# K^T V moved behind the attention products, these done in quarter arrays, and K and V loaded ahead of Q

## Chip, cores, metric

One core of one Trainium2 chip. The metric is the device time of one execution in microseconds (us).

## The reference

```python
kv  = np.einsum('bhsd,bhse->bhde', k, v)        # 8 batches, 8 heads, 576 rows, 64 wide
out = np.einsum('bhsd,bhde->bhse', q, kv)
rms = np.sqrt(np.mean(out * out, axis=-1, keepdims=True) + 1e-06)
x   = (out / rms * g_norm)                      # then heads side by side: 4608 x 512
h   = x @ w_in                                  # 512 x 2048
g   = np.where(h > 0, h, np.exp(np.minimum(h, 0)) - 1)
return g @ w_out                                # 2048 x 512
```

Nearly all the arithmetic is in the last two matrix products; the attention is many small ones.

## The kernel before

The kernel works on nine tiles of 512 rows. Window T runs the two big products of tile T and T-1 and, in their midst, the attention of tile T+1. Every window is a list of steps in TensorE's order:

- `M3B`: the first product for two of 16 column blocks of tile T (8 full matmuls) into PSUM pair B (A, B, C are the pairs), `E3` the vector part of its elu. `R` instead of `M` lets ScalarE take the relu, which makes that vector part shorter.
- `H5`, `h0`: half of an output block of the second product for tile T-1 or T (8 full matmuls). The last half of a block is followed by ScalarE's copy, and every second block by a store.
- `K5C`: K^T V of batch 5 into pair C. `XA`: the two attention products of tile T+1 into pairs A and C, with squares, sums and inverse roots. `Y`: the scaling and the transposes of x, issued by the sync engine. `G0`, `G1`: multiply the transposed halves by g. `Q`: transposes of the next batch's q, a small copy on GpSimd (the gate) that waits until they have landed, and behind it the loads of the batch after.

```python
def fetch_ahead(b):
    raw[b] = stage.tile([P, 4, RK, D], FP32, name="st_q", tag="q")
    load(raw[b], "q", b)
    for name in "kv":
        fetch(name, b)

def kv_mm(b, kv_ps, u, ls=range(2)):            # quarter arrays: 64 rows x 64 columns
    for j in range(RK):
        for s in range(2):
            rows = slice(s * 64, s * 64 + 64)
            for l in ls:
                nc.tensor.matmul(kv_ps[s][l * 64 : l * 64 + 64, u * 64 : u * 64 + 64],
                    lhsT=bf["k", b][rows, 2 * l + u, j, :], rhs=bf["v", b][rows, 2 * l + u, j, :],
                    start=(j == 0), stop=(j == RK - 1))

def se_mm(T, h, se_ps):                         # half arrays, quarters where two batches meet
    for i in range(2):
        (b0, j0), (b1, j1) = (slot_of(T, 4 * h + 2 * i + t) for t in range(2))
        parts = [(0, P, b0, j0, 2)] if b0 == b1 else [(0, 64, b0, j0, 1), (64, P, b1, j1, 1)]
        ...                                     # for m, for l, for part: one matmul of 64 columns

steps = "M0B K5C H1 E0 M1A H3 E1 M2B H4 E2 H5 XA Y H6 Q M3B H7 E3 M4A E4 M5C E5 M6B G0 E6 M7A G1 E7 h0 h2"   # window 4
```

Of the kernel before, what the change touches and what calls it, by code (L numbers as in the profile page):

```python
# [8 lines left out]
FP32 = mybir.dt.float32  # L9
# [7 lines left out]
def kernel(  # L17
# [14 lines left out]
    P = 128  # L32

    B, H, S, D = q.shape
    DM = H * D
    DF = moe_w_in.shape[1]
    RK = S // 64
# [5 lines left out]
    V, A, Q = nc.vector, nc.scalar, nc.gpsimd  # L43

    const = ctx.enter_context(tc.tile_pool(name="const", bufs=1))
    stage = ctx.enter_context(tc.tile_pool(name="stage", bufs=1))
# [28 lines left out]
    def slot_of(T, n):  # L75
        return divmod(8 * T + n, RK)

    bf, raw = {}, {}
    src_of = {"q": q, "k": k, "v": v}

    def fetch(name, b, u=None):

        if (name, b) not in bf:
            bf[name, b] = qkvp.tile([P, 4, RK, D], BF16, name=f"{name}_bf", tag=name)
        ms = slice(0, 4) if u is None else slice(u, 4, 2)
        load(bf[name, b][:, ms], name, b, ms)

    def load(dst, name, b, ms=slice(0, 4), eng=nc.gpsimd):
        in_ = src_of[name][b].rearrange("h r d -> (h r d)").rearrange("(m p x) -> p m x", m=4, p=P)
        eng.dma_start(out=dst.rearrange("p m j d -> p m (j d)"), in_=in_[:, ms, :])  # L90

    def fetch_ahead(b):
        raw[b] = stage.tile([P, 4, RK, D], FP32, name="st_q", tag="q")
        load(raw[b], "q", b)
        for name in "kv":
            fetch(name, b)

    def cast_q(b):

# [67 lines left out]
    def kv_of(b, l, u, s):  # L167
        return kv_sb[l * 64 : l * 64 + 64, b, u, s]
# [11 lines left out]
    def y_mm(T, u, ps, ls=range(2)):  # L180

        n = 0
        while n < 8:
            b, j = slot_of(T, n)
            m = min(8 - n, RK - j)
            for l in ls:
                for s in range(2):
                    nc.tensor.matmul(  # L188
                        ps[l][s * 64 : s * 64 + 64, n * 64 : (n + m) * 64],
                        lhsT=kv_of(b, l, u, s),  # L190
                        rhs=qT[b][l * 64 : l * 64 + 64, s, u, j : j + m, :],
                        start=True,
                        stop=True,
                    )
            n += m
# [19 lines left out]
    class Turned:  # L215
# [7 lines left out]
        def product(self, y):  # L223
            self.y = y
            y_mm(self.T, self.u, y)
# [11 lines left out]
        def scale(self, l):  # L237
            scale_t(self.T, self.y[l], self.r[:, l, :], 2 * l + self.u)

    def se_mm(T, h, se_ps):  # L240

        for i in range(2):
            (b0, j0), (b1, j1) = (slot_of(T, 4 * h + 2 * i + t) for t in range(2))
            parts = [(0, P, b0, j0, 2)] if b0 == b1 else [(0, 64, b0, j0, 1), (64, P, b1, j1, 1)]
            for m in range(4):
                u, s = m // 2, m % 2
                for l in range(2):
                    for lo, hi, b, j, n in parts:
                        nc.tensor.matmul(  # L249
                            se_ps[lo:hi, l, (4 * i + m) * 64 : (4 * i + m) * 64 + 64],  # L250
                            lhsT=qT[b][l * 64 : l * 64 + 64, s, u, j : j + n, :],
                            rhs=kv_of(b, l, u, s),
                            start=True,
                            stop=True,
                        )

    def kv_all(b, tag):
        kv_ps = pair(tag, "kv_ps")
        for u in range(2):
            kv_mm(b, [kv_ps[:, s, :] for s in range(2)], u)  # L260
        return lambda: nc.scalar.copy(
            kv_sb[:, b], kv_ps[:, :, 0:P].rearrange("p s (u e) -> p u s e", u=2)
        )

    def attention(T):

        st = {}

        def se(h):
            def product(tag="C"):  # L270
                st["se", h] = pair(tag, "se_ps")
                se_mm(T, h, st["se", h])

            def square():
                sq = attp.tile([P, 2, DM], BF16, name="sq", tag="sq")
                nc.scalar.activation(sq, st["se", h], AF.Square)  # L276
                st["sq", h] = sq

            def sums():
                ss = attp.tile([P, 2 * H], FP32, name="ss", tag="ss")  # L280
                st["ss", h] = ss
                nc.vector.reduce_sum(  # L282
                    out=ss,
                    in_=st.pop(("sq", h)).rearrange("p l (m e) -> p (l m) e", e=D),
                    axis=AX.X,
                )

            def inv():
                ss = st["ss", h]
                nc.scalar.activation(ss, ss, AF.Ln, bias=eps_col, scale=1.0 / D)  # L290
                nc.scalar.activation(ss, ss, AF.Exp, scale=-0.5)  # L291

            def scale():
                if h == 0:
                    st["xs"] = attp.tile([P, J, DM], BF16, name="xs", tag="xs")
                    x_tile(T)
                se_ps, ss = st.pop(("se", h)), st.pop(("ss", h))
                nc.vector.tensor_tensor(  # L298
                    out=st["xs"][:, 2 * h : 2 * h + 2, :].rearrange("p i (l m e) -> p l i m e", l=2, e=D),
                    in0=se_ps.rearrange("p l (i m e) -> p l i m e", i=2, e=D),  # L300
                    in1=ss.rearrange("p (l i m) -> p l i m", l=2, i=2).unsqueeze(4).to_broadcast([P, 2, 2, 4, D]),
                    op=ALU.mult,
                )
                for i in (2 * h, 2 * h + 1):
                    nc.sync.dma_start_transpose(
                        out=xT[T][:, :, i * P : i * P + P], in_=st["xs"][:, i, :]
                    )

            def gain():
                cols = slice(2 * h * P, 2 * h * P + 2 * P)  # L310
                nc.vector.tensor_scalar(  # L311
                    out=xT[T][:, :, cols],
                    in0=xT[T][:, :, cols],
                    scalar1=g_col,
                    scalar2=None,
                    op0=ALU.mult,
                )

            return product, square, sums, inv, scale, gain

        pieces = {}
        for h in range(2):
            for name, piece in zip(("se", "sq", "sum", "inv", "mul", "gain"), se(h)):
                pieces[f"{name}{h}"] = piece
        return pieces
# [124 lines left out]
    def mm2_half(T, i):  # L450
        mm2(T, i // 2, 8 * (i % 2), 8 * (i % 2) + 8)
# [90 lines left out]
    y_ps, sq0 = {}, {}  # L542
# [217 lines left out]
    def window(T, steps):  # L760





        rest = {}
        nxt = attention(T + 1) if T + 1 < NT else None
        for step in steps.split():
            kind, arg = step[0], step[1:]
            if kind in "MR":  # L770
                i, tag = int(arg[0]), arg[1]
                make = mm1_rest if T == 2 and i == 0 else mm1
                rest[i] = make(T, i, tag, kind == "R")
            elif kind == "E":
                rest.pop(int(arg))()
            elif kind == "H":
                mm2_half(T - 1, int(arg))
            elif kind == "h":
                mm2_half(T, int(arg))
            elif kind == "K":  # L780
                kv_all(int(arg[0]), arg[1])()
            elif kind == "X":
                nxt["se0"](arg)
                nxt["se1"]("C")
                for name in ("sq0", "sq1", "sum0", "sum1", "inv0", "inv1"):
                    nxt[name]()
            elif step == "Y":
                nxt["mul0"]()
                nxt["mul1"]()
            elif step == "Q":  # L790
                b = T + 2
                if b < B:
                    turn_q(b)
                if b + 1 < B:
                    after_turn(b)
                    fetch_ahead(b + 1)
            elif kind == "G":
                nxt[f"gain{arg}"]()
            else:
                raise ValueError(step)  # L800
# [4 lines left out]
    for T in range(2, NT):  # L805
        if T + 2 < B:
            cast_q(T + 2)
        if T == 2:
            steps = "M0B K3C E0 M1A H5 E1 M2B E2 R3A H6 E3 XB Y H7 Q M4A E4 h0 R5B E5 M6C G0 E6 M7A G1 E7 h2"
        elif T + 1 < NT:  # L810
            kv = f"K{T + 1}C" if T + 1 < B else ""
            steps = (
                f"M0B {kv} H1 E0 M1A H3 E1 M2B H4 E2 H5 XA Y H6 Q M3B H7 E3 M4A E4 M5C E5 M6B G0 E6 M7A G1 E7 h0 h2"
            )
        else:
            steps = "M0B H1 E0 M1A H3 E1 M2B H4 E2 M3A H5 E3 M4B H6 E4 M5A H7 E5 M6B E6 M7A E7 h0 h2"
        window(T, steps)
# [33 lines left out]
```

## Time and profile before

| | before |
|---|---|
| median of the runs in the first comparison | 284.10 us |
| span of the core in the profile | 282.2 us |
| PE busy | 273.3 us, 97% |
| waits of PE for another engine after 50 us | none listed |

The span runs from the core's first instruction to its last; the time adds some 1.8 us around it. PE is TensorE's matmuls. Two figures from single matmul starts are used throughout: the **cost of a piece** (last full matmul before it to a full one after it, less 216 ns per full step) and the **inner distance**, from the last full matmul before window 2's product to that before window 7's: 142.17 us before. It leaves out the start of the kernel, which the change does not touch and which shifts by up to 0.6 us between traces.

### The profile page before, as it was taken

What the parts mean: (1) busy time and instruction counts of PE and PEld (TensorE: products, weight loads), DVE (VectorE), ACT (ScalarE), POOL (GpSimd) and SP (SyncE); (2) the same over time, 40 slices, a digit from 0 to 9 for tenths busy, and PEclk for the clock granted to TensorE, in tenths of its full rate; (3) what the DMA queues carried; (4) which work ended last, traced back from release to release, by engine and by line L of the source; (5) the groups of instructions that cost most, each with busy time, mean ns of one, the idle gap of its engine ahead of it and who ended that gap; (6) DMA issues with size and microseconds to landing.
All of it is one profiled execution on the core that took longest, in us unless ns stands there. A gap on an engine that the chain in (4) does not pass through costs nothing.

```text
span 282.2 us, 5145 instructions
## 1 busy us (share of the span) xinstructions
PE 273.3 (97%) x2094; PEld 129.2 (46%) x2123; DVE 163.9 (58%) x222; ACT 141.6 (50%) x209; POOL 49.1 (17%) x89
## 2 busy tenths in 40 slices
PE   8799999999999999999999999999999999999994
PEld 3444444444544444444444444444444444444443
DVE  2549532967457736864587448834893489344600
ACT  3778359594566445533552445344543464333311
POOL 7743303322033033034003400000000000000000
PEclk9999999999999999999999999999999999999999
DMA  7999999999999969579437954612180215030222
GB/s 207 201 204 206 206 258 238 196 254 121 173 277 178 155 186 232 99 193 261 108 74 175 268 130 42 148 49 74 37 114 0 74 40 112 0 77 1 74 74 74
DMA packets 50571, 39.46 MB, mean 140 GB/s; under 512 B 30964, under 2 KB 44020, under 8 KB 50548
## 3 DMA queue, kind: packets, MB, share of 16 engines
q0 software_dynamic: 15008, 21.30, 37.6%
q1 hardware_dynamic: 35136, 17.31, 29.9%
q10 hardware_dynamic: 404, 0.53, 0.6%
q8 instruction: 16, 0.26, 0.3%
q14 instruction: 7, 0.06, 0.1%
HBM read 36.70 MB, written 9.44 MB: 163 GB/s over the span
## 4 chain that ended last, share of the span: by engine, by line
PE 92%; DMA 3%; POOL 1%; issue 1%; ACT 1%; DVE 1%; POOLq 0%; DVEq 0%
PE h_ps L381 42%; PE o_ps L402 42%; DMA v_bf<-in_v_dram 3%; PE kv_ps L155 2%; PE se_ps L249 2%; PE h_ps L568 1%; PE o_ps L439 1%; POOL k_bf L90 1%; PE qt_ps L173 0%; PE mean L198 0%; PE y_ps L188 0%; POOL v_bf L90 0%; ACT elu_e L349 0%; DVE xT L211 0%; POOL q_bf L90 0%
## 5 line engine op out<-in xcount | busy, mean ns | idle before, releaser
L402 PE MATMUL o_ps<-w_out_sb,gT 128*128 128x512 bf16 x542 | 127.1, 379 | 1.5 <-issue 1.0
L381 PE MATMUL h_ps<-xT,w_in_sb 128*128 128x512 bf16 (+1 forms) x551 | 125.5, 376 | 0.6
L349 ACT ACTIVATE elu_e<-h_ps 128x1024 bf16<-128x1024 f32 (+1 forms) x79 | 73.9, 951 | 73.0 <-PE h_ps L381 71.6
L381 PEld LDWEIGHTS <-w_in_sb 128*128 128x128 bf16 x560 | 54.5, 98 | 64.5 <-issue 0.9
L402 PEld LDWEIGHTS <-gT 128*128 128x128 bf16 x560 | 53.5, 98 | 64.0 <-issue 0.9
L365 DVE TENSOR_TENSOR gT<-elu_e,h_ps 128x1024 bf16<-128x1024 bf16 (+1 forms) x67 | 77.2, 1157 | 6.9 <-DVE elu_e L361 0.5
L361 DVE TENSOR_SCALAR elu_e<-elu_e 128x1024 bf16<-128x1024 bf16 x72 | 32.0, 445 | 59.1 <-ACT elu_e L349 59.0
L418 ACT COPY o_sb<-o_ps 128x512 f32<-128x512 f32 x32 | 18.3, 586 | 30.8 <-PE o_ps L402 30.8
L103 POOL CAST q_bf<-st_q 128x384 bf16<-128x384 f32 x36 | 18.0, 544 | 39.1 <-DMA st_q<-in_q_dram 34.4
L282 DVE TENSOR_REDUCE ss<-sq 128x16 f32<-128x1024 bf16 x14 | 16.5, 1214 | 13.0 <-ACT sq L276 13.0
L298 DVE TENSOR_TENSOR xs<-se_ps,ss 128x1024 bf16<-128x1024 f32 x14 | 16.5, 1216 | 1.2 <-ACT ss L291 1.2
L276 ACT ACTIVATE sq<-se_ps 128x1024 bf16<-128x1024 f32 x14 | 13.7, 1030 | 0.3 <-PE se_ps L249 0.3
L211 DVE SCALAR_TENSOR_TENSOR xT<-y_ps,g_col,rT 128x512 bf16<-128x512 f32 (+1 forms) x10 | 6.2, 640 | 10.1 <-ACT rT L208 8.0
L338 POOL COPY gate<-qT 1x16 bf16<-1x16 bf16 x5 | 0.9, 186 | 57.3 <-DMA qT<-q_bf 57.3
L354 ACT ACTIVATE elu_h<-h_ps 128x1024 bf16<-128x1024 f32 (+1 forms) x12 | 9.3, 817 | 0.0
L155 PEld LDWEIGHTS <-k_bf 64*64 64x64 bf16 x576 | 6.3, 107 | 5.3 <-issue 5.3
L155 PE MATMUL kv_ps<-v_bf,k_bf 64*64 64x64 bf16 x576 | 7.5, 194 | 1.0 <-DVE v_bf L112 0.5
L90 POOL DMA_DIRECT2D v_bf<-in_v_dram x11 | 7.7, 698 | 4.0 <-DMA w_in_sb<-in_moe_w_in_dram 2.1
L90 POOL DMA_DIRECT2D k_bf<-in_k_dram x11 | 7.8, 705 | 2.7 <-DMA w_in_sb<-in_moe_w_in_dram 2.0
L290 ACT ACTIVATE ss<-ss,eps_col 128x16 f32<-128x16 f32 x14 | 4.3, 307 | 6.7 <-DVE ss L282 6.7
L365 DVE TENSOR_TENSOR gT<-elu_e,elu_h 128x1024 bf16<-128x1024 bf16 x9 | 6.6, 739 | 1.6 <-ACT elu_h L354 0.9
L311 DVE TENSOR_SCALAR xT<-xT,g_col 128x1024 bf16<-128x1024 bf16 x14 | 6.7, 481 | 1.2 <-DMA xT<-xs 1.2
(56 smaller groups left out, 92.9 us busy)
## 6 DMA issues: line engine op xcount, KB each, us to landing
st_q<-in_q_dram POOLq DMA_DIRECT2D x6, 1152.0 KB, 7.9
out_dram<-o_sb SPq DMA_DIRECT2D x24, 256.0 KB, 3.3
k_bf<-in_k_dram POOLq DMA_DIRECT2D x6, 576.0 KB, 10.4
v_bf<-in_v_dram POOLq DMA_DIRECT2D x6, 576.0 KB, 12.7
out_dram<-o_sb SPq DMA_DIRECT2D x19, 128.0 KB, 2.4
w_out_sb<-in_moe_w_out_dram POOLq DMA_DIRECT2D x4, 512.0 KB, 15.1
w_in_sb<-in_moe_w_in_dram POOLq DMA_DIRECT2D x2, 512.0 KB, 10.8
q_bf<-in_q_dram POOLq DMA_DIRECT2D x3, 288.0 KB, 13.6
```

Source lines behind the costliest of these rows:

```text
L90: eng.dma_start(out=dst.rearrange("p m j d -> p m (j d)"), in_=in_[:, ms, :])
L103: nc.gpsimd.tensor_copy(out=bf["q", b][:, u, js], in_=raw[b][:, u::2, js, :].rearrange("p l j d -> p j l d"),)
L155: nc.tensor.matmul(kv_ps[s][l * 64 : l * 64 + 64, u * 64 : u * 64 + 64], lhsT=bf["k", b][rows, 2 * l + u, j, :], rhs=bf["v", b][rows, 2 * ...
L276: nc.scalar.activation(sq, st["se", h], AF.Square)
L282: nc.vector.reduce_sum(out=ss, in_=st.pop(("sq", h)).rearrange("p l (m e) -> p (l m) e", e=D), axis=AX.X,)
L298: nc.vector.tensor_tensor(out=st["xs"][:, 2 * h : 2 * h + 2, :].rearrange("p i (l m e) -> p l i m e", l=2, e=D), in0=se_ps.rearrange("p l ...
L349: nc.scalar.activation(e[:, lo:hi, :], h, AF.Exp)
L361: nc.vector.tensor_scalar(out=e, in0=e, scalar1=1.0, scalar2=1.0, op0=ALU.min, op1=ALU.subtract)
L365: nc.vector.tensor_tensor(out=gT[T][:, 2 * i + lo : 2 * i + hi, :], in0=e[:, lo:hi, :], in1=h, op=ALU.add if relu else ALU.max,)
L381: nc.tensor.matmul((ps[a] if isinstance(ps, list) else ps[:, a, :])[:, cols], lhsT=w_in_sb[:, c, f * P : f * P + P], rhs=xT[T][:, c, cols] ...
L402: nc.tensor.matmul(o_ps[T, j], lhsT=gT[T][:, f, j * P : j * P + P], rhs=w_out_sb[:, f, :], start=(f == 0), stop=(f == FC - 1),)
L418: nc.scalar.copy(o_sb[T, half][:, j % 2, :], o_ps[T, j])
```

## The change

The intent is to spare TensorE its changes of array mode. K^T V of batches 5 to 7 goes directly behind the two attention products of windows 3 to 5, one window earlier than it was, and the products there (and in the even windows, where a pair of rows crosses a batch) use quarter arrays all through. K and V are then wanted a window earlier, so they are loaded ahead of their Q.

```diff
-    def fetch_ahead(b):
-        raw[b] = stage.tile(...); load(raw[b], "q", b)
-        for name in "kv":
-            fetch(name, b)
+    def fetch_ahead(b, order="qkv"):
+        for name in order: ...
-            parts = [(0, P, b0, j0, 2)] if b0 == b1 else [(0, 64, b0, j0, 1), (64, P, b1, j1, 1)]
+            parts = [(0, 64, b0, j0, 1), (64, P, b1, j1, 1)]
+            if b0 == b1 and not quarters:
+                parts = [(0, P, b0, j0, 2)]
             elif kind == "X":
-                nxt["se0"](arg)
-                nxt["se1"]("C")
+                quarters = len(arg) > 1 or T % 2 == 0
+                nxt["se0"](arg[0], quarters)
+                nxt["se1"]("C", quarters)
+                nxt["sq0"]()
+                if len(arg) > 1:
+                    kv_all(int(arg[1]), arg[2])()
-                    fetch_ahead(b + 1)
+                    fetch_ahead(b + 1, "kvq")
+        elif T == 3:
+            steps = "M0B K4C H1 E0 M1A H3 E1 M2B H4 E2 M3A H5 E3 H6 XB5A Y H7 Q M4A E4 h0 M5B E5 M6C G0 E6 M7A G1 E7 h2"
         elif T + 1 < NT:
-            kv = f"K{T + 1}C" if T + 1 < B else ""
-            steps = f"M0B {kv} H1 E0 M1A ... H5 XA Y H6 Q M3B ... h0 h2"
+            kv = f"{T + 2}B" if T + 2 < B else ""
+            steps = f"M0B H1 E0 M1A ... H5 XA{kv} Y H6 Q M3B ... h0 h2"
```

(The code is shortened: the calls after K^T V are the squares, sums and inverse roots as before. The step lists are cut at the dots; the rest of them is unchanged.)

More of the change, by code (lines that the diff above doesn't have):

```diff
@@ L90, in load @@
         eng.dma_start(out=dst.rearrange("p m j d -> p m (j d)"), in_=in_[:, ms, :])
-    def fetch_ahead(b):
-        raw[b] = stage.tile([P, 4, RK, D], FP32, name="st_q", tag="q")
-        load(raw[b], "q", b)
-        for name in "kv":
-            fetch(name, b)
+    def fetch_ahead(b, order="qkv"):
+        for name in order:
+            if name == "q":
+                raw[b] = stage.tile([P, 4, RK, D], FP32, name="st_q", tag="q")
+                load(raw[b], "q", b)
+            else:
+                fetch(name, b)
     def cast_q(b):
@@ L238, in scale, with se_mm @@
             scale_t(self.T, self.y[l], self.r[:, l, :], 2 * l + self.u)
-    def se_mm(T, h, se_ps):
+    def se_mm(T, h, se_ps, quarters=False):
         for i in range(2):
             (b0, j0), (b1, j1) = (slot_of(T, 4 * h + 2 * i + t) for t in range(2))
-            parts = [(0, P, b0, j0, 2)] if b0 == b1 else [(0, 64, b0, j0, 1), (64, P, b1, j1, 1)]
+            parts = [(0, 64, b0, j0, 1), (64, P, b1, j1, 1)]
+            if b0 == b1 and not quarters:
+                parts = [(0, P, b0, j0, 2)]
             for m in range(4):
@@ L269, in se, with product @@
         def se(h):
-            def product(tag="C"):
+            def product(tag="C", quarters=False):
                 st["se", h] = pair(tag, "se_ps")
-                se_mm(T, h, st["se", h])
+                se_mm(T, h, st["se", h], quarters)
             def square():
@@ L782, in window @@
             elif kind == "X":
-                nxt["se0"](arg)
-                nxt["se1"]("C")
-                for name in ("sq0", "sq1", "sum0", "sum1", "inv0", "inv1"):
+                quarters = len(arg) > 1 or T % 2 == 0
[4 more added lines that the diff above has]
+                    kv_all(int(arg[1]), arg[2])()
+                for name in ("sq1", "sum0", "sum1", "inv0", "inv1"):
                     nxt[name]()
@@ L809 @@
             steps = "M0B K3C E0 M1A H5 E1 M2B E2 R3A H6 E3 XB Y H7 Q M4A E4 h0 R5B E5 M6C G0 E6 M7A G1 E7 h2"
+        elif T == 3:
+            steps = "M0B K4C H1 E0 M1A H3 E1 M2B H4 E2 M3A H5 E3 H6 XB5A Y H7 Q M4A E4 h0 M5B E5 M6C G0 E6 M7A G1 E7 h2"
         elif T + 1 < NT:
-            kv = f"K{T + 1}C" if T + 1 < B else ""
-            steps = (
-                f"M0B {kv} H1 E0 M1A H3 E1 M2B H4 E2 H5 XA Y H6 Q M3B H7 E3 M4A E4 M5C E5 M6B G0 E6 M7A G1 E7 h0 h2"
-            )
+            kv = f"{T + 2}B" if T + 2 < B else ""
+            steps = f"M0B H1 E0 M1A H3 E1 M2B H4 E2 H5 XA{kv} Y H6 Q M3B H7 E3 M4A E4 M5C E5 M6B G0 E6 M7A G1 E7 h0 h2"
         else:
```

## The prediction

> **What bounds the kernel now.** I read the page's busy row first, then the waits of TensorE over the steady part, then the chain that ended last, and last the single matmul starts.
>
> ```profile
> span 282.2 us, 5145 instructions
> PE 273.3 (97%) x2094; PEld 129.2 (46%) x2123; DVE 163.9 (58%) x222; ACT 141.6 (50%) x209; POOL 49.1 (17%) x89
> PEclk9999999999999999999999999999999999999999
> ```
>
> 97% busy alone would prove little. The wait list of PE from 50 us to the end does:
>
> ```profile
> engine line waited for: us in total, times, longest us
> PE o_ps L402 <- issue: 0.8, 5, 0.2
> ```
>
> In 232 us PE waits for no other engine long enough to be listed. So what the change adds to or takes from PE's stream shows one to one in the time, unless it makes a new wait. The chain (start, duration, work) shows the pieces concerned:
>
> ```profile
> 108.13 0.57 PE se_ps L249 x32
> ...
> 124.35 1.73 PE h_ps L381 x8
> 126.07 0.71 PE kv_ps L155 x72
> 126.78 0.16 issue
> 126.94 1.67 PE o_ps L402 x7
> ...
> 137.24 0.81 PE se_ps L249 x40
> ```
>
> L155 is K^T V of a batch (72 matmuls, 64x64 arrays), alone between full matmuls. L249 is the attention product (both halves of a tile): 32 matmuls on 64x128 half arrays, or 40 where a pair of rows crosses a batch, 16 of which are on 64x64 quarters between half-array ones.
>
> Single starts in the trace give the rates. Full matmuls: 216 ns apart. Half arrays: two in 29 ns. Quarters: four in 32 ns (8 each). A change of mode costs a start-to-start of 120 to 125 ns; from a full matmul to a small one it is 309 to 312 ns instead of 216. What a piece costs is the distance from the last full matmul before it to a full one after it, less 216 ns per full step (a few records are missing and are counted in):
> - K^T V alone: 811 ns = 96 entry + 582 for its 72 + 133 exit (windows 4, 5, 6 alike).
> - product on halves, no crossing (windows 3, 5): 680 ns.
> - product with a crossing: 915 and 916 ns (windows 2, 4), 809 in window 6, where the quarters come last and one switch is saved.
>
> **What the Trainium skill says.** "TensorEngine Tiling (Array Packing)", Key Properties: changing the tiling mode drains the array, changing only the tile does not. The trace agrees: 120 to 125 ns at a switch against 26 within a mode. "TensorE: Matmul & The Clock Gate", Part 3, says small tiles of different row groups overlap and start about 4 ns apart; here the four of a quarter group start 3 to 4 ns apart, the groups 32 ns. "DMA: Bandwidth & Descriptors", Issuing engines are not separate DMA queues: all DMAs share 16 engines and interleave. The trace agrees: with an output store in flight, K and V packets land at 48 to 60 per 0.5 us (108 to 110.5 us), without one at 83 to 93 (111 to 112.5). The two mode rules are why the change can pay, the last is its risk.
>
> **The change, part by part.**
> It removes the separate K^T V of batches 5, 6, 7 (3 x 811 ns), puts the same matmuls behind the products of windows 3, 4, 5, and makes the products of windows 2 to 6 all quarters: 64 instead of 32 or 40 small matmuls, 136 more in all. At 8 ns a quarter, 64 need what 32 halves need, so doubling the count is free. Taking the K^T V figure as template: 64 quarters alone (8 fewer) cost 811 - 8 x 8 = 747 ns; 64 + 72 cost 811 + 64 x 8 = 1323 ns.
> - Window 2: 915 to 747, -168.
> - Window 3: 680 + 811 to 1323, -168.
> - Window 4: 916 + 811 to 1323, -404.
> - Window 5: 680 + 811 to 1323, -168.
> - Window 6: 809 to 747, -62.
> - Sum: **-0.97 us**, all on PE, which is the path.
>
> ACT's copy of K^T V (0.37 us) now sits between the two squares. The vector work needs the first square and then 1.2 us for its sum, so the second sum starts about when it did: no cost.
>
> Added wait 1, end of window 3. Its new order puts the product late, as window 2 has it, with only seven groups of eight full matmuls after it. Window 2 already pays for this:
>
> ```profile
> 94.49 0.48 DVE L311 TENSOR_SCALAR xT<-xT,g_col 128x1024 bf16<-128x1024 bf16 x1
> ...
> 95.07 1.89 PE L381 MATMUL h_ps<-xT,w_in_sb 128*128 128x512 bf16 x8
> ```
>
> The last gain ends at 94.97, the next window's first matmul starts at 95.07, 456 ns after the one before it instead of 216: 0.24 us of waiting. Window 3 gets no relu form for its tile 5, so the product of that elu takes 1.22 us on DVE instead of 0.69. Counted from the first product matmul: tile 5's exp at 8.32, min 9.38, product 9.90, gain 11.04, min 11.43, product 11.96, second gain 13.10 to 13.58, matmul at 13.68; PE would be ready at 13.31. **+0.37 us**, in a window that had no such wait.
>
> Added wait 2, K and V of batch 6 in window 4. Loads go out when GpSimd's gate sees Q's transposes landed:
>
> ```profile
> 99.73 0.19 POOL L338 COPY gate<-qT 1x16 bf16<-1x16 bf16 x1 [12.28 <-DMA qT<-q_bf]
> ...
> 122.13 0.19 POOL L338 COPY gate<-qT 1x16 bf16<-1x16 bf16 x1 [11.56 <-DMA qT<-q_bf]
> ```
>
> ```profile
> 92.31 1.29 SPq L460 DMA_DIRECT2D out_dram<-o_sb  x2
> 93.69 3.73 SPq L330 DMA_TRANSPOSE qT<-q_bf  x2
> ...
> 118.42 2.83 SPq L330 DMA_TRANSPOSE qT<-q_bf  x2
> ```
>
> In window 2 a store goes just ahead of the transposes and the gate opens 6.0 us after their issue; in window 3, with the store behind them, 3.7 us. In the new order of window 3 the eighth half (H7), hence its store, comes ahead, so I take 6.0. Window 3's first product matmul: 94.90 + 72 x 0.2158 + 0.81 + 0.10 = 111.34 us. In window 2 the gate came 17.7 us after that point, so here at 129.0; K goes out at 129.6, first packets 2.3 us after that (as 100.27 to 102.5 showed), 1024 packets of K and V at 85 to 90 per 0.5 us take 5.8 us, and the next tile's store from about 134.3 on takes some 1.2 us more: V lands at 138 to 139.2. Window 4 wants it at 125.02 + 56 x 0.2158 + 0.10 + 0.52 = 137.7. So **0 to 1.5 us** of waiting; loading K and V ahead of Q is what keeps it from being several. Batch 5 has about 2 us to spare (V landed near 109.5 to 110, wanted at 111.9), batch 7 about 5. Q lands last but is cast long before its transposes.
>
> Sum without wait 2: 284.08 - 0.97 + 0.37 = 283.48. With 0.8 us of it: 284.3.
>
> **The rivals.**
> (a) Pure PE arithmetic, both waits absent: 283.1. For it: everything listed of PE's waits is tiny, and the odd order of window 3 looks made to let batch 5 land. Against it: window 2's own 0.24 us wait has the same cause.
> (b) The load of batch 6 comes late by its full estimate or more: 284.9 to 285.3. For it: both windows with a store ahead of Q's transposes (gates at 77.15 and 99.73) took 6.0 us, the three others 3.6 to 3.7. Against it: about 1.1 us of these 6.0 is a pause of the transposes that may not recur, and the estimate's errors are as large as the wait.
> (c) Quarters lose: K^T V's stationary operand, or the second bank, brings a pause between product and K^T V, 0.1 us at each of three places: +0.3. Both use the same four arrays in the same order, so I give it little.
>
> **Range and chances.** Between 283.5 (no late load) and 284.3 (late by 0.8) I lean slightly to the middle: **283.9 us**. Range 283.1 (rival a) to 285.1 (rival b). No path reaches 2% (5.7 us): faster 0.01, same 0.98, slower 0.01.
>
> **What would show it.** Right: the K^T V groups of batches 5 to 7 gone as separate pieces; in the chain a product of 64 and K^T V of 72 in one stretch of some 1.1 us in windows 3, 4 and 5, quarters at 8 ns each; no 120 ns jump inside windows 2 to 6. Wait 1: a gap of about 0.4 us at window 4's first h_ps matmul, released by DVE L311. Wait 2: PE kv_ps waiting on a v_bf or k_bf DMA near 137.7 us; the gate near 129 confirms its cause, a gate near 127 refutes it. Wrong would be: a quarter rate well off 8 ns when the moving operand is kv_sb in long runs, a wait on PSUM tile A or B in window 3 (I count 1 us of slack for the bank of tile 3), or a load that misses batch 5 as well.

## The result, and the profile after

284.43 us (284.34 to 285.28, 4 runs) against 284.10 (283.95 to 284.42, 4 runs). The ratio is 1.0017, interval 0.9996 to 1.0038: the same within 2%, slightly slower if anything. Ratios here are the mean time of one kernel's runs over that of the other's of the same rounds, so not quite the ratio of the medians quoted.

The waits of PE after 50 us, in the kernel after:

```profile
engine line waited for: us in total, times, longest us
PE o_ps L407 <- issue: 0.5, 3, 0.2
PE h_ps L386 <- DVE xT L316: 0.2, 1, 0.2
```

L316 is the multiplication by g. That is a wait on another engine, which the kernel before did not have in this list. The chain of the kernel after shows where (start, duration, work):

```profile
111.81 0.64 PE se_ps L254 x64
112.45 0.74 PE kv_ps L157 x72
113.20 0.16 issue
113.36 1.67 PE o_ps L407 x7
...
123.89 0.06 DVE gT L370
123.95 1.08 issue
125.03 0.49 DVE xT L316
125.52 0.05 issue
125.57 1.90 PE h_ps L386 x8
...
137.83 0.64 PE se_ps L254 x64
138.47 0.04 issue
138.51 0.77 PE kv_ps L157 x72
```

The first lines are the new piece in window 3: 64 quarter matmuls of the product with the 72 of K^T V behind. In the middle the chain leaves PE for DVE: the first matmul of window 4 starts 560 ns after the matmul before it, 344 more than the usual 216. In the last lines there is a hole ahead of K^T V of batch 6. The views name no releaser for so short a hole, but the semaphores' times do. K^T V starts 61 ns after the product's last matmul where it waits for nothing (window 5). In window 3 it was 158: 15 of the 16 completion updates of V's load had come by 111.81 us, the last at 112.29. In window 4 it was 229: 15 by 137.70, the last at 138.38.

| ns | before | forecast | after |
|---|---|---|---|
| window 2, product | 915 | 747 | 748 |
| window 3, product and K^T V of 5 | 680 + 811 | 1323 | 1491, of which 97 for V |
| window 4, product and K^T V of 6 | 916 + 812 | 1323 | 1561, of which 168 for V |
| window 5, product and K^T V of 7 | 680 + 811 | 1323 | 1397 |
| window 6, product | 809 | 747 | 746 |
| wait for the gain, window 4 | 0 | 370 | 344 |

The sums are 6434 before and 6287 after: 0.15 us less, and the inner distance is 142.03 us, 0.14 less. So this trace's middle is a little faster; its window 2 began 0.40 us later for reasons ahead of the change, and its span is 282.5 us. Of the 0.97 us that the forecast saves on PE only 0.14 arrived. The experiments ask what the rest depends on.

### The profile page after: what moved, and what is told of

It reads as the page before. It is cut to its first block, busy times and chain, and to the rows that moved or that the text cites. A ratio compares the mean times of both kernels' runs of the same rounds, so it can differ in the third digit from the quotient of the medians.

```text
span 282.5 us, 5417 instructions
## 1 busy us (share of the span) xinstructions
PE 273.9 (97%) x2229; PEld 129.6 (46%) x2259; DVE 163.0 (58%) x222; ACT 142.0 (50%) x209; POOL 48.2 (17%) x89
## 4 chain that ended last, share of the span: by engine, by line
PE 94%; DVE 2%; issue 2%; ACT 1%; DVEq 0%
PE o_ps L407 42%; PE h_ps L386 41%; PE kv_ps L157 2%; PE se_ps L254 2%; PE kv_ps L529 2%; PE h_ps L573 1%; PE o_ps L444 1%; PE qt_ps L175 1%; ACT elu_e L354 1%; PE mean L200 1%; PE y_ps L190 1%; DVE elu_e L366 0%; DVE xT L316 0%; DVE kv_sb L114 0%; DVE xT L213 0%
## 5 line engine op out<-in xcount | busy, mean ns | idle before, releaser
L366 DVE TENSOR_SCALAR elu_e<-elu_e 128x1024 bf16<-128x1024 bf16 x72 | 31.0, 431 | 59.0 <-ACT elu_e L354 58.9
L105 POOL CAST q_bf<-st_q 128x384 bf16<-128x384 f32 x36 | 16.7, 508 | 61.0 <-DMA st_q<-in_q_dram 55.6
L316 DVE TENSOR_SCALAR xT<-xT,g_col 128x1024 bf16<-128x1024 bf16 x14 | 6.9, 491 | 1.8 <-DMA xT<-xs 1.8
## 6 DMA issues: line engine op xcount, KB each, us to landing
out_dram<-o_sb SPq DMA_DIRECT2D x19, 128.0 KB, 2.4
```

The source lines that it names most:

```text
L105: nc.gpsimd.tensor_copy(out=bf["q", b][:, u, js], in_=raw[b][:, u::2, js, :].rearrange("p l j d -> p j l d"),)
L366: nc.vector.tensor_scalar(out=e, in0=e, scalar1=1.0, scalar2=1.0, op0=ALU.min, op1=ALU.subtract)
```

## The experiments

Each edit is relative to the kernel after, unless it says otherwise. All results were correct. "Before" is the kernel before on the same chip, 11 runs per batch: 284.07, 284.08 and 284.17 us median in the three batches.

### after_again: no edit

> The changed kernel as it is, beside the others on the same chip. My theory: TensorE's stream is 0.9 us shorter, and 0.7 to 0.8 us of it is given back by three waits that the change makes: the first matmul of window 4 waits about 0.34 us for the second gain of xT, and K^T V of batches 5 and 6 wait 0.1 and 0.2 us for the last of V. So 0.0 to 0.3 us over the kernel before, with these waits in the trace again, the two for V of varying length. Rival (run-to-run start only): the waits are not there again and the time equals before less 0.9.

284.99 us (283.72 to 285.77), ratio 1.0033 (1.0015 to 1.0052). The profiled run was the shortest; in its trace batch 5 waited for nothing (60 ns), batch 6 began 206 ns after the product, the gain was waited for as before, and the inner distance was 141.91 us. The waits are there, and the unprofiled runs are 1 to 2 us longer than the profiled one. The kernel before never scattered so: 283.76 to 284.39.

### quarters_only: the products alone

```diff
 # relative to before: quarters in windows 2 to 6, all else as before
+ quarters = T < 7
```

> The kernel before with nothing but the quarter arrays in the products of windows 2 to 6; K^T V, the loads and the order of window 3 are as before. My sum of mode switches says -168 (window 2), +67 (3), -169 (4), +67 (5), -62 (6) = -0.27 us against before, products of 747 ns each. Rival: twice as many small matmuls cost time in themselves; then windows 3 and 5 lose 0.3 us each and the total is not below before.

Each of the five products cost 745 to 748 ns, and the inner distance was 141.90 us, 0.26 under before: the sum held. A view of its chain:

```profile
108.06 0.64 PE se_ps L254 x64
```

This stands against x32 in 0.57 us for window 3 before. Twice the matmuls take 67 ns more by the starts (747 against 680 ns), so windows 3 and 5 lose and only the three crossings gain. The timed runs did not show the 0.26: 284.10 us, ratio 1.0005 (0.9993 to 1.0017). Its spans had a mean of 282.12 against 282.27, and the time outside the span was 1.76 to 2.72 us against 1.74 to 1.82 in before; the last section comes back to this.

### turn_before_store: Q's transposes ahead of the store

```diff
-"... XB Y H7 Q M4A ..."    "... XB5A Y H7 Q M4A ..."     # windows 2 and 3
+"... XB Y Q H7 M4A ..."    "... XB5A Y Q H7 M4A ..."
```

> The changed kernel with Q's transposes issued ahead of half H7 (and so ahead of its store) in windows 2 and 3. If the late V is due to the gate that waits behind the store, the gates come 3.7 us after the transposes' issue instead of 5 to 6, K and V land 2 us earlier and both waits of K^T V vanish: 0.3 us under the changed kernel, the wait for the gain (0.34) stays. Rival: the 16 DMA engines are simply full, the store then falls into the loads, V lands no earlier and the waits stay.

Two lines of the timeline of window 3 in the kernel after (start, duration, engine, work), and the same two of this one:

```profile
123.58 3.52 SPq L335 DMA_TRANSPOSE qT<-q_bf  x2
...
128.57 0.47 POOL L343 COPY gate<-qT 1x16 bf16<-1x16 bf16 x1 [10.70 <-DMA qT<-q_bf]
```

```profile
121.75 2.80 SPq L335 DMA_TRANSPOSE qT<-q_bf  x2
...
125.46 0.19 POOL L343 COPY gate<-qT 1x16 bf16<-1x16 bf16 x1 [8.86 <-DMA qT<-q_bf]
```

The gate comes 3.7 us after the transposes' issue instead of 5.0 (in window 2, 3.6 instead of 6.3). So the store ahead does delay the transposes. But beside after_again, whose window 2 began within 0.06 us of this one, V of batch 6 was issued 2.5 us earlier and landed only 1.1 us earlier (136.70), and V of batch 5 was issued 3.9 earlier and landed 0.9 earlier (110.71): the store now runs beside the loads. In the trace the waits for V were gone (78, 60 and 61 ns), inner distance 141.78. The time was 284.26 us (283.63 to 286.32), ratio 1.0018 (0.9994 to 1.0042): both theory and rival got a part right, and the scatter stayed.

### only_6_7: batch 5 and window 3 as before

```diff
-steps = "M0B K4C ... M3A H5 E3 H6 XB5A Y H7 Q ... h2"      # window 3
+steps = "M0B K4C H1 ... H5 XA Y H6 Q ... h0 h2"            # window 3 as before
+"M0B K5C H1 ..."                                           # window 4: batch 5 alone
```

> Only batches 6 and 7 are moved behind the products of windows 4 and 5; window 3 keeps the order and the halves of before, and batch 5 stays alone at the start of window 4. By my sum: window 2 -0.17, window 4 -0.33, window 5 -0.09, window 6 -0.06 = -0.65 us against before, no wait for the gain in window 4 and none for V. Rival: if moving K^T V behind the product saves nothing in itself, the result stays within 0.2 us of before.

283.48 us (283.24 to 283.54, and one run of 284.80 with a span of 283.0), ratio 0.9987 (0.9971 to 1.0003): the median is 0.59 under before, but the interval still takes in no change. The inner distance was 141.53 us, 0.635 under before, against 0.65 by the sum. V of batch 6 landed at 134.66, wanted at 137.7: window 3's gate opens early when its store is behind the transposes. No wait for the gain in window 4. So in the trace moving batches 6 and 7 pays what the arithmetic says, and what costs goes with batch 5 and window 3's new order. The one long run was not traced; V of batch 6 had 3 us to spare in the run that was, so a late V is no ready reason for it.

### q_load_first: the old order of loads

```diff
-fetch_ahead(b + 1, "kvq")
+fetch_ahead(b + 1, "qkv")
```

> The changed kernel with the old order of loads (Q, then K, V) in the windows. If the load of V stands right at the edge, V of batch 5 lands near 114.5 us (as in the kernel before) against 112.2 wanted, and V of batch 6 near 142 against 138.2 plus the delay so far: K^T V waits about 2.3 and 4 us, the time is 5 to 7 us over the changed kernel, some 290 us. Rival: V has slack and the spread of the changed kernel has another cause; then the order of loads changes under 1 us.

293.60 us, ratio 1.0334 (1.0320 to 1.0349): worse than forecast. Waits of PE, and the granted clock (the column after the engines) in two stretches of this kernel:

```profile
PE kv_ps L157 <- DMA v_bf<-in_v_dram: 5.5, 2, 3.0
```

```profile
core 0: us, PE busy (x) PEld busy (x) DVE busy (x) ACT busy (x) POOL busy (x), PEclk, DMA share, GB/s
114.50:118.50 4.00, 3.67 (x79) 1.84 (x81) 1.84 (x2) 2.23 (x6) 0.00 (x0) 0.58 0.01 4
119.00:125.00 6.00, 6.00 (x29) 2.74 (x28) 2.79 (x4) 2.42 (x3) 0.00 (x0) 1.00 0.43 87
```

V of batch 5 landed at 114.36 us and K^T V began 2.73 us after the product; in window 4, 3.17 us. The waits were forecast, their price was not: after each, the granted clock was 0.50 for 3.41 us (from 115.16 and from 145.88 us; the 0.58 above is the mean of a stretch that begins before it), and eight full matmuls took 427 ns apiece instead of 216, about 1.7 us more per wait. The Trainium skill, "TensorE: Matmul & The Clock Gate", Why this matters for your kernels, says to leave no PE gaps over about 3 us between bursts, or the clock goes back to half; here 2.73 us from start to start, some 2.5 us of it idle, was enough, while gaps of 1.94 and 1.61 us (gain_earlier and both_mended) left the clock at 1.00. The load order in the change is therefore worth about 9 us: without it the move would have been a clear loss.

### gain_earlier: the second gain ahead of the sixth elu

```diff
-"... M6C G0 E6 M7A G1 E7 h2"      # windows 2 and 3
+"... M6C G0 G1 E6 M7A E7 h2"
```

> The changed kernel with the second gain issued ahead of the sixth elu's vector work in windows 2 and 3. My theory: the waits of 0.24 us (window 3's first matmul) and 0.34 us (window 4's) vanish, so 0.58 us under the changed kernel of the same rounds, the waits for V stay or grow by what PE arrives earlier (up to 0.58 us given back to them). Rival: the gain waits for its transposes instead, the gaps stay as they are.

284.80 us (284.45 to 286.19), ratio 1.0036 (1.0017 to 1.0056). Both gaps at the first matmuls of windows 3 and 4 vanished. But PE then came to K^T V of batch 6 earlier, and V came later (139.11). The chain of this trace goes straight from the load to K^T V:

```profile
129.20 9.91 DMA v_bf<-in_v_dram
139.11 0.14 issue
139.24 0.77 PE kv_ps L157 x72
```

K^T V began 1.94 us after the product. Most of that is one of the load's 16 completions: fifteen had come by 137.76, the last at 139.11. The 0.58 us saved were more than given back: the load did not come earlier for it, so taking away the wait ahead of it gained nothing.

### kv_window_earlier and kv_earlier_gain: K and V one window earlier still

```diff
-qkvp = ... tc.tile_pool(name="qkvp", bufs=3)
+qkvp = ... tc.tile_pool(name="qkvp", bufs=4)
 # fetch_ahead(4) loads batch 4 and K, V of 5; later ones load Q of b and K, V of b + 1
+        if 4 <= b < B - 1:
+            for name in "kv":
+                fetch(name, b + 1)
 # kv_earlier_gain: also the edit of gain_earlier
```

> The changed kernel with K and V loaded one window earlier still (a fourth buffer for each), so that neither can be waited for; the wait for the gain is left in. My theory: K^T V of batches 5 to 7 starts 61 ns after the product in each window (a semaphore instruction remains), the distance from window 2's product to window 7's is 141.7 us against 142.17 before, the time is about 0.4 us under before and the spread of the runs (283.7 to 285.8 for the changed kernel) shrinks to that of before (some 0.6 us). Rival: the spread and the loss come from elsewhere, and both stay.

> Both mends: K and V one window earlier, and the second gain ahead of the sixth elu in windows 2 and 3. My sum: -0.97 of the change, -0.24 of the wait that the kernel before has in window 3, +0.2 for three semaphore instructions: 1.0 us under before, 283.1 us. Rival: what is taken away shows up as another wait (transposes for the gain, loads that collide with stores), under 0.5 us of gain.

291.20 us, ratio 1.0269 (1.0248 to 1.0290), and 290.01, ratio 1.0216 (1.0198 to 1.0235). The waits for V were gone, as the theory said: product and K^T V together cost 1397 ns in windows 3 to 5 of the first one. But the extra loads (K and V of batch 5 on top of the three of batch 4) filled the DMA engines just when x is transposed for window 3. Waits of PE in kv_window_earlier, and the gain's line there:

```profile
PE h_ps L389 <- DVE xT L319: 5.7, 2, 5.5
```

```profile
97.76 0.49 DVE L319 TENSOR_SCALAR xT<-xT,g_col 128x1024 bf16<-128x1024 bf16 x1 [5.35 <-DMA xT<-xs]
```

One gain idled 5.35 us for its transposes (landing took up to 9.3 us, median 2.5), PE 5.5 us behind it, and the clock fell again. This experiment removed one wait and made another, so it cannot say where the scatter comes from; its runs lie 2.1 us apart with no wait for V in the trace. The rival of kv_earlier_gain (collisions) won.

### after_third: no edit

> The changed kernel a third time, for the spread and for one more trace. In the traces so far K^T V of batch 6 began 229 and about 200 ns after the product (61 is the least), while most unprofiled runs were 0.5 to 1.5 us longer. Theory: the same wait for V of batch 6, of 0 to 2 us; so runs between 283.7 and 286, and the profiled run's time over the shortest equals its gap before that K^T V. Rival: a long run shows no such gap.

284.54 us (283.79 to 285.31), ratio 1.0014 (0.9999 to 1.0028). The profiled run was once more the shortest: K^T V began 98 ns after the product in window 3, 248 in window 4. No long run of the kernel after itself was caught in a trace.

### only_5_7: batch 6 alone taken back

```diff
-kv = f"{T + 2}B" if T + 2 < B else ""
+kv = "7B" if T == 5 else ""
+"M0B K6C H1 ..."                    # window 5: batch 6 alone
```

> The changed kernel with batch 6 alone taken back (its K^T V stands at the start of window 5, in no hurry for its V); window 3 keeps its new order with batch 5. My sum: -168 (window 2), -94 (3), -168 (4), -94 (5), -62 (6), +343 for the gain = -0.24 us against before, with 0 to 0.2 us for V of batch 5; and if V of batch 6 makes the spread, the runs lie within some 0.6 us of each other as before's do. Rival: batch 5 or something else makes the spread: it stays 1.5 us or more and the time at 284.5 or over.

284.24 us (283.79 to 285.53), ratio 1.0016 (0.9998 to 1.0035). The inner distance was 141.925 us, 0.241 under before: the sum to a hundredth. But the scatter stayed, with spans of 281.9 to 283.6. So V of batch 6 is not its only source. V of batch 5 is another candidate: it landed at 111.40 us for 111.7. But the traced run had no wait, so that is not shown.

### only_6_7_gain: only 6 and 7, and the gain earlier in window 2

```diff
 # only_6_7, and in window 2:
-"... M6C G0 E6 M7A G1 E7 h2"
+"... M6C G0 G1 E6 M7A E7 h2"
```

> Batches 6 and 7 moved, window 3 as before, and in window 2 the second gain issued ahead of the sixth elu's vector work, which takes away the 0.24 us that the kernel before waits too. My sum: -0.65 - 0.24 = -0.89 us against before, 283.2 us, the fastest of all. Rival: the 0.24 us come back at another wait; then it is as only_6_7 was, 0.6 us under before.

283.30 us (283.11 to 283.37), ratio 0.9969 (0.9957 to 0.9980): 0.9 us under before, the fastest of all and with the least scatter. The inner distance is 141.27 us, 0.895 less than before, against 0.89 by the sum. Its timeline of the gain in window 2 and the next matmul:

```profile
93.62 0.48 DVE L316 TENSOR_SCALAR xT<-xT,g_col 128x1024 bf16<-128x1024 bf16 x1 [0.70 <-DMA xT<-xs]
...
94.84 1.89 PE L386 MATMUL h_ps<-xT,w_in_sb 128*128 128x512 bf16 x8
```

The gain now idles 0.70 us for its transposes, but ends 0.74 us ahead of the matmul, and PE no longer waits.

### both_mended: all three batches, store and gain mended

```diff
 # the edits of turn_before_store and gain_earlier together
```

> The changed kernel with all three batches moved, Q's transposes ahead of H7's store and the second gain earlier, both in windows 2 and 3. By the traces V of batch 6 then lands at 136.7 us against 137.3 wanted, V of batch 5 at 110.7 against 111.6: my sum is -0.97 - 0.24 + 0.2 = -1.0 us against before in a run with no wait, but with only 0.6 us to spare and a landing that scatters by 1 us many runs should lose up to 1 us, so a median near 283.7 and a spread over 1 us. Rival: the traces' slack holds and all runs lie near 283.1.

284.83 us (283.87 to 286.79), ratio 1.0026 (1.0002 to 1.0051). The scatter is over 1 us as expected, the median worse than expected. In its trace V of batch 6 landed at 138.76 us, 2 us later than in turn_before_store although issued 0.2 earlier, and K^T V began 1.61 us after the product. For this load a landing is uncertain by more than the slack that these orders give it. The run of 286.79 us was not traced, but its granted clock is 0.994, where every other run of these orders but q_load_first and the two with K and V a window earlier has 0.997 or more; the traced run of kv_earlier_gain, with one stretch at half clock behind a gap, has 0.993. That points to a long gap of PE in it, and does not show which.

## Why the prediction was right or wrong

The time lay in the range: 283.9 forecast, 284.43 measured, 283.1 to 285.1 given. The direction did not: 0.2 us under before was forecast, 0.33 over was measured, and part of that comes from outside the core's span, for which the prediction has no term. By its own steps:

- **PE's stream, -0.97 us.** Right for the products alone (748 and 746 ns against 747). For product and K^T V it was 1397 against 1323 ns: K^T V starts 61 ns after the product's last matmul where a step of 8 was assumed, and the 64 quarters take 525 ns from first start to last, not 504. So the stream alone gives -0.75, not -0.97. A semaphore instruction of 51 ns stands in PE's queue in that pause; that it makes the pause was not tested. This is the size of rival (c), to which little was given: its 0.1 us per place was near the 0.074 measured, though its two reasons were not tested either. The sentence that doubling the count is free was wrong by the prediction's own figures (64 quarters at 8 ns are 512 ns, 32 halves at 14.5 are 464), but its sum used 747 against 680 and so was not touched. (By the starts K^T V alone is 93 + 582 + 136 ns, not 96 + 582 + 133; its 811 is right.)
- **Wait 1, +0.37 us for the gain.** Right: 0.34 in all three traces of the kernel after. The cause is shown by gain_earlier, which removes it.
- **Wait 2, 0 to 1.5 us for V of batch 6.** The mechanism was right, shown by the semaphores' times, by q_load_first and by the chain of gain_earlier. That the landing fitted (137.8 to 138.4 us for 138 to 139.2) is partly luck: the gate came at 128.0 to 128.6 instead of 129.0, because the transposes took 4.9 to 5.0 us behind the store and not 6.0, and the first packets came at 130.0 to 130.5 instead of 131.9, but the packets then took 7.4 to 7.6 us and not 5.8, or 7.0 with a store beside them. In the kernel's own traces the wait was 0.15 to 0.19 us, where the forecast leant on 0.8; in two edited orders that reach K^T V earlier it was 1.55 and 1.88.
- **"Batch 5 has about 2 us to spare"** was wrong. V landed at 111.6 to 112.3 us, not at 109.5 to 110. The first packets came at 102.0 to 102.5, as counted on, but the 1024 packets of K and V took 9.1 to 9.5 us: 48 to 57 per 0.5 us in the first 3 us, and 42 to 53 for some 2 us beside a store, where the prediction counts 85 to 90 for batch 6. It stood at the edge: 0 to 0.1 us of wait in the traces.
- **What the timed runs add.** The 16 runs of the kernel after have a mean span of 282.64 us against 282.32 for 33 runs of before. A run with no wait for V would have, by the corrected sum, about 282.32 - 0.75 + 0.34 = 281.9, which is the shortest span seen. So 0.74 us on average are lost beyond the shortest. That this is V in every long run was argued from the two edited orders; no long run of the kernel after was traced, and the long runs of only_6_7 and only_5_7 speak against V of batch 6 as the only source. The time outside the span adds 0.3 us on average that nothing in the prediction had; its cause stays open.

So where did the gain go? 0.22 us was never there, 0.34 went into the gain's wait that the new order of window 3 brings, and in the three traces 0.15 to 0.27 into V of batches 5 and 6, which land just as they are wanted. What the rest of the 0.74 us and the 0.3 us outside the span come from is not shown.

## What to carry to other kernels

Count what a regrouping of small matmuls saves from single starts: in four traces here sums of 0.24 to 0.89 us held to two hundredths of a microsecond. But a consumer moved a window earlier is only as fast as its load. Measure the load's landing over several runs: here landings of one load in nearly equal orders lay 2 us apart, and 3 us of slack left no wait in the two traces that had it. Taking back the one move without slack, and window 3's new order with it, turned a loss of 0.1 to 0.3% into a saving of 0.1% that is not clear of noise; with the multiplication by g issued earlier in window 2 as well it became 0.3%, which is. And when two waits follow one another on the same engine and the later one is for a load that does not depend on the earlier, removing the earlier one only lengthens the later, as in gain_earlier.

## What the Trainium skill lacked or had wrong

- "TensorEngine Tiling (Array Packing)", Key Properties, says that a change of mode drains, without a size. Here: 118 to 127 ns from start to start instead of 26 to 32; 309 to 312 instead of 216 when coming from a full matmul.
- "TensorE: Matmul & The Clock Gate", Back-to-back issue gap, gives about 25 ns as the least step for a matmul of up to 64 columns. The starts on one tile were 29 to 32 ns apart here; but over four quarters in rotation the mean step was 8 ns, over two halves 14.5.
- The same page, Why this matters for your kernels, puts the limit for PE gaps at about 3 us: a gap of 2.73 us from start to start (some 2.5 us idle) was followed by 3.41 us at half clock; gaps of 1.94 and 1.61 us were not.
- No page gives a size for the scatter of one load's 16 completions: the last came 0.48 and 0.68 us after the fifteenth in the two late loads of the kernel after, 1.35 us in gain_earlier.
- No page says what a store queued ahead of transposes within SBUF costs: 4.9 to 6.3 us from issue to the gate instead of 3.6 to 3.7.
- No page explains why the time outside the core's span varies: 1.73 to 1.83 us in 33 runs of the kernel before and at most 1.84 in 11 runs of only_6_7 and only_6_7_gain, but 1.74 to 2.87 in the 16 of the kernel after, over 1.84 in 8 of them, and up to 2.72 in quarters_only, whose loads are those of before.
